# Eight experts served in the order of their counts, with a fixed room for each place of that order

## The chip, the cores and the metric

One core of one Trainium2 chip runs the whole kernel. The metric is the device time of the launch in microseconds (us). Times are medians over several launches of the same build. PE is the matrix engine (PEld its weight loads), DVE the vector engine, ACT the scalar engine, POOL the general engine that also issues indirect gathers, and SP the engine that issues plain DMA transfers.

## What is computed

Three layers, one behind the other. First a retention attention (4 batches, 8 heads, 576 positions, head size 64). Its output, 2304 tokens of 512 numbers, goes through a mixture of 8 experts of which each token uses the best two, and the result of that through a wide layer with `h * cos(h)`.

```python
logits = x @ w_gate                                   # 2304 x 8
noisy = logits + np.log1p(np.exp(x @ w_noise)) * noise
top2 = np.argpartition(-noisy, 2, axis=1)[:, :2]
top2_w = softmax(noisy[top2])
for e in range(8):
    for k in range(2):
        mask = top2[:, k] == e                        # how many: known only at run time
        h = np.maximum(x[mask] @ w1[e], 0.0)          # 512 -> 1024
        out[mask] += top2_w[mask, k, None] * (h @ w2[e])
h = out @ w_in                                        # 512 -> 2048
return (h * np.cos(h)) @ w_out                        # 2048 -> 512
```

Which tokens go to which expert, and how many, depends on the data. Together there are 4608 assignments, 576 for each expert on average.

## The kernel before, in words

**Numbers.** Each fp32 product is made from split values: a number is a high part and a low part, and one product takes three matmul passes (high by high, and the two mixed ones, `PASSES`). Weights arrive as units of 128x1024 fp32 (512 KB) in three staging buffers. `load_unit` (L273, on SP) asks for the next one, `split_unit` makes the high part on ACT (L286) and the low part on DVE (L287) and then asks for another. An expert has eight units, a0 to a3 of `w1` and b0 to b3 of `w2`.

**Attention and routing.** Twenty tiles run through attention. `routing(gi)` works beside it on four groups of tiles and finds, for each token, its two experts, their weights and its place within each expert. The last group ends with the tables of all experts: `ptab` to `gidx` (L668, whole rows of expert 0) and `gf` (L672), which a matmul spreads (L531) into `gidx4` (L683) for the gathers by quarter rows. Behind them two small matmuls (L686, L687) give the counts `cnt` (L688), from which `ntot` (L691) is the number of extra turns for tokens beyond an expert's room.

**Experts.** Every expert has a room of fixed size: `CAP = 616` columns, tokens being columns of the matmuls. A room is worked as two groups: group 0 with 256 columns (320 for expert 0) and group 1 with the rest, 360 (296 for expert 0). The number of columns is part of the instruction, so all of the room is computed, whether it holds tokens or not. `layer1(e, g)` makes 8 steps of 12 matmuls (L817), `layer2(e, g)` 4 steps of 24 (L838), so that a group takes 192 matmuls and an expert 384. Tokens are brought by gathers on POOL (`gather`, L730 and L736) and turned on PE (`turn`, L784). Between the steps of one expert stand the gathers and turns of the next, the splitting of its weights, and some steps of `cg`, which first computes `slot` (where each token's two results lie, `final_slots`, L1080 to L1110) and then prepares the last layer's weights (`convs`). The results go to DRAM as `ys` (L851 full blocks of 32 rows, L855 the rest of a room).

**Extra turns.** `overflow` (L995) reads `ntot` into a register and runs one turn of 128 tokens for each that does not fit a room. It stands between expert 0's first half and expert 0's second.

**The end of the experts.** The last expert (7) runs layer 1 and layer 2 of group 0, then `fetch(0)` starts 16 gathers from `ys` (L1171) for the first two blocks of tokens; these read only the rows up to the end of expert 7's group 0 (`FIRST`). Beside them PE runs group 1 of expert 7. `turn2(0)` weighs and adds the fetched rows (L1189, L1190), and `mlp1` (L1211 to L1229) and `mlp2` (L1241) follow for each of nine pairs of blocks.

**What sets the order.** Nothing is planned at run time. The order on every engine is that of the program, and the small work beside the matmuls is put in by hand-written lists of step numbers (`CG_1`, `CG_2`, `TURN_AT` and others).

Of the kernel before, what the change touches and what calls it, by code (L numbers as in the profile page):

```python
# [27 lines left out]
NTILE = B * NC  # L28
# [3 lines left out]

CAP = 616
NB = 5
CUT0, CUT = 320, 256
ROOM = (CUT0, CAP - CUT)
XB = (N - 512) // 128
YR = E * CAP
RB = N // 128
# [76 lines left out]
def constants():  # L116
    gam = 1.0 - 2.0 ** (-5.0 - np.arange(H, dtype=np.float64))
    pos = np.arange(S, dtype=np.float64)
    up = gam[:, None] ** pos[None, :] / np.sqrt(D)
    dn = gam[:, None] ** (-pos[None, :])  # L120
    dq = np.zeros((128, HP, 128), np.float32)
    gs = np.zeros((128, NC - 1, HP), np.float32)
    for hp in range(HP):
        for s in range(2):
            dq[s * 64:(s + 1) * 64, hp] = up[2 * hp + s, :128]
            for c in range(1, NC):
                gs[s * 64:(s + 1) * 64, c - 1, hp] = gam[2 * hp + s] ** START[c]
# [17 lines left out]
    xb[:, 0] = CAP  # L145
# [8 lines left out]
    small = np.concatenate([xb, io, base, k[:, None], k[:, None] // 32, tok, it], 1)  # L154

    spread = np.zeros((128, 4, 128), np.float32)
    for g in range(4):
        spread[:, g] = k[:, None] == g * 32 + (k % 32)[None, :]
    return {"c_dq": dqs, "c_big": big.astype(np.float32), "c_small": small.astype(np.float32),
            "c_spread": spread.reshape(128, -1), "c_zero": np.zeros((128, DM), np.float32)}  # L160
# [3 lines left out]
       ("strict", 128)]  # L164
SMALL = [("xb", E * XB), ("io", E), ("base", GN * E), ("pi", 1), ("pa", 1), ("tok", NTILE), ("it", E * RB)]

# [44 lines left out]
def moe_kernel(ctx, tc, x, out, dbg=None, phases="ABC"):  # L211
# [35 lines left out]
    cnt = con.tile([128, E], F32, name="cnt")  # L247
    ntot = con.tile([128, 1], I32, name="ntot")
    cbias = con.tile([128, 2], F32, name="cbias")
    beat = con.tile([1, 1], F32, name="beat")  # L250
# [3 lines left out]

    units = []
    for e in range(E):
        units += [(f"a{j}", x["w1"][4 * (e or E) + j], [128, DC, 256]) for j in range(4)]
        units += [(f"b{j}", x["w2"][4 * e + j], [128, 2, DM]) for j in range(4)]
# [3 lines left out]
    state.update(load=0, split=0, a=wpa)  # L262

# [114 lines left out]
    run = rt.tile([128, E], BF, name="run")  # L378
    adj = rt.tile([128, E], BF, name="adj")
    ptab = ps.tile([128, E * RB], F32, name="ptab")  # L380
    lgs = []
# [152 lines left out]
    ranked, begun = [0], []  # L534

    def routing(gi):

# [143 lines left out]
        if gi == len(GRP) - 1:  # L681
            pq = spread_out(gf.rearrange("p e n -> p (e n)"), "ph", PHB)
            vec.tensor_scalar(gidx4, pq, 4.0, sl["pa"], op0=OP.mult, op1=OP.add)  # L683
            yield
            pn = ps.tile([128, E], F32, name="ph", bufs=PHB)
            nc.tensor.matmul(pn, ones, run, start=True, stop=False)  # L686
            nc.tensor.matmul(pn, ones, adj, start=False, stop=True)  # L687
            vec.tensor_copy(cnt, pn)  # L688
            xf = rt.tile([128, E * XB], F32, name="xf", bufs=1)
            vec.tensor_tensor(ev(xf), ev(sl["xb"]), cnt[:, :, None].to_broadcast([128, E, XB]), op=OP.is_lt)  # L690
            vec.tensor_reduce(ntot, xf, axis=AX.X, op=OP.add)  # L691
            yield
# [31 lines left out]
    def gather(e, blk, early=False):  # L724
# [9 lines left out]
        else:  # L734
            ix = egid[:, blk:blk + 1] if early else gidx[:, e * RB + blk:e * RB + blk + 1]
            nc.gpsimd.indirect_dma_start(out=t.rearrange("p a d -> p (a d)"), out_offset=None,  # L736
# [8 lines left out]
    def width(e, g):  # L745
        cut = CUT if e else CUT0
        return CAP - cut if g else cut

    def places(e, blk):

        cut = CUT if e else CUT0
        c0, c1 = blk * 128, min(blk * 128 + 128, CAP)
        if c0 < cut:
# [73 lines left out]
    def layer2(e, g, early=False):  # L827
# [4 lines left out]
        for c in range(DC):  # L832
# [13 lines left out]
            if c < DC - 1:  # L846
                yield
        r0 = e * CAP + g * width(e, 0)
        for a in range(4):
# [222 lines left out]
    def final_slots():  # L1072
# [11 lines left out]
        for e in range(1, E):  # L1084
# [16 lines left out]
        V.scalar_tensor_tensor(ov, ei, float(CAP - N), vf, op0=OP.mult, op1=OP.add)
        V.tensor_tensor(slot.rearrange("p k t -> p (k t)"), a, ov, op=OP.add)
        yield
# [55 lines left out]

    FIRST = (E - 1) * CAP + 256  # L1160

# [198 lines left out]
```

## Time and profile before

| | |
|---|---|
| median of 3 runs | 980.35 us |
| the three runs | 980.35, 976.11, 986.68 us |
| the profiled execution | 986.75 us |
| its span in the trace | 985.0 us |
| its mean granted clock of TensorE | 0.988 |
| PE busy | 954.1 us (97%) |
| PEld busy | 894.9 us (91%) |
| DVE busy | 681.9 us (69%) |
| POOL busy | 485.6 us (49%) |
| ACT busy | 371.8 us (38%) |

The profiled execution is one execution, and 6.4 us longer than the median of the three runs. The share of busy time is a mean over stages that have different limits, so a stage has to be read by itself. Attention takes the first 145 us or so, the experts the time to about 570 us, the last layer the rest.

### The profile page before, as it was taken

What the parts mean: (1) busy time and instruction counts of PE and PEld (TensorE: products, weight loads), DVE (VectorE), ACT (ScalarE), POOL (GpSimd) and SP (SyncE); (2) the same over time, 40 slices, a digit from 0 to 9 for tenths busy, and PEclk for the clock granted to TensorE, in tenths of its full rate; (3) what the DMA queues carried; (4) which work ended last, traced back from release to release, by engine and by line L of the source; (5) the groups of instructions that cost most, each with busy time, mean ns of one, the idle gap of its engine ahead of it and who ended that gap; (6) DMA issues with size and microseconds to landing.
All of it is one profiled execution on the core that took longest, in us unless ns stands there. A gap on an engine that the chain in (4) does not pass through costs nothing.

```text
span 985.0 us, 18025 instructions
## 1 busy us (share of the span) xinstructions
PE 954.1 (97%) x6853; PEld 894.9 (91%) x6853; DVE 681.9 (69%) x1366; ACT 371.8 (38%) x659; POOL 485.6 (49%) x549
## 2 busy tenths in 40 slices
PE   8988988999999999999999899999999999999998
PEld 6776888999999999999999897989898998989897
DVE  4799875586878878686964378767484848566671
ACT  2422413341414232332333255435353535344451
POOL 6453114461818365473812537474654637473621
PEclk9998997999999999999999999999999999999999
DMA  9987495476758667686835342110101010111110
GB/s 348 283 280 211 117 356 168 129 220 172 240 165 238 210 194 218 171 259 167 252 95 155 122 134 89 36 36 33 55 15 51 20 46 25 44 32 40 30 23 22
DMA packets 79353, 135.39 MB, mean 137 GB/s; under 512 B 13025, under 2 KB 43105, under 8 KB 79265
## 3 DMA queue, kind: packets, MB, share of 16 engines
q1 hardware_dynamic: 69648, 113.74, 37.3%
q0 software_dynamic: 9472, 20.20, 7.3%
q8 instruction: 55, 0.90, 0.4%
q10 hardware_dynamic: 144, 0.27, 0.1%
q14 instruction: 34, 0.27, 0.1%
HBM read 106.25 MB, written 35.26 MB: 144 GB/s over the span
## 4 chain that ended last, share of the span: by engine, by line
PE 84%; DVE 6%; DMA 4%; issue 2%; POOL 1%; another core or an unknown queue 1%; ACT 1%; SPq 1%; DVEq 0%; ACTq 0%; POOLq 0%
PE py L1241 18%; PE ph L838 12%; PE ph L817 10%; PE ph L1211 10%; PE pt L817 8%; PE pt L1211 6%; PE ptab L817 4%; PE pt L838 3%; PE ptab L1211 3%; PE ptab L838 3%; DMA st<-w 2%; PE ph L446 1%; PE py L474 1%; PE py L488 1%
## 5 line engine op out<-in xcount | busy, mean ns | idle before, releaser
L1171 POOL DMA_INDIRECT y<-ys,slot x144 | 139.3, 967 | 53.9 <-issue 25.8
L1229 POOL TENSOR_TENSOR gl<-t,gh 128x512 fp32r<-128x512 f32 x67 | 87.0, 1300 | 136.4 <-issue 95.1
L730 POOL DMA_INDIRECT rows<-xs,gidx x132 | 134.8, 1021 | 35.0 <-issue 28.1
L743 POOL COPY beat<-hh 1x1 f32<-1x1 f32 x120 | 55.4, 462 | 154.7 <-ACT hh L822 150.6
L838 PE MATMUL ph<-hh,hb 128*128 128x360 f32 (+2 forms) x312 | 95.8, 307 | 1.7 <-issue 1.7
L838 PE MATMUL ph<-hh,lb 128*128 128x360 f32 (+2 forms) x312 | 96.1, 308 | 0.4 <-issue 0.4
L838 PE MATMUL ph<-hl,hb 128*128 128x360 f32 (+2 forms) x312 | 95.9, 307 | 0.6 <-issue 0.5
L1190 DVE SCALAR_TENSOR_TENSOR y<-y,wts,y 128x128 f32<-128x128 f32 x72 | 39.1, 579 | 55.4 <-DMA y<-ys,slot 46.0
L1217 DVE TENSOR_SCALAR t<-t 128x512 f32<-128x512 f32 x72 | 35.0, 486 | 49.3 <-ACT t L1216 49.3
L1219 DVE TENSOR_SCALAR t<-t 128x512 int32<-128x512 int32 x72 | 66.9, 930 | 2.5
L761 ACT ACTIVATE xh<-xt 128x512 fp32r<-128x512 f32 (+1 forms) x33 | 20.3, 616 | 114.4 <-DVE xt L769 107.1
L1222 ACT ACTIVATE t<-t,cbias 128x512 f32<-128x512 f32 x72 | 52.0, 722 | 29.0 <-DVE t L1219 27.8
L1241 PE MATMUL py<-ld,gh 128*128 128x512 f32 (+1 forms) x152 | 57.9, 381 | 3.7 <-POOL ld L287 2.5
L838 PEld LDWEIGHTS ph<-hh,hb 128*128 128x128 f32 x312 | 59.1, 189 | 2.1 <-issue 2.1
L838 PEld LDWEIGHTS ph<-hh,lb 128*128 128x128 f32 x312 | 59.1, 189 | 1.7 <-issue 1.7
L838 PEld LDWEIGHTS ph<-hl,hb 128*128 128x128 f32 x312 | 59.2, 190 | 0.1
L1241 PE MATMUL py<-hb,gh 128*128 128x512 f32 (+1 forms) x152 | 58.3, 384 | 0.0
L1241 PE MATMUL py<-lb,gh 128*128 128x512 f32 (+1 forms) x152 | 58.3, 383 | 0.0
L1241 PE MATMUL py<-hb,gl 128*128 128x512 f32 (+1 forms) x152 | 58.2, 383 | 0.0
L1241 PE MATMUL py<-hd,gh 128*128 128x512 f32 (+1 forms) x152 | 57.5, 378 | 0.0
L1241 PE MATMUL py<-hd,gl 128*128 128x512 f32 (+1 forms) x152 | 57.5, 378 | 0.0
L287 DVE TENSOR_TENSOR la<-st,ha 128x1024 fp32r<-128x1024 f32 x36 | 44.8, 1244 | 12.2 <-ACT ha L286 11.8
(308 smaller groups left out, 2657.5 us busy)
## 6 DMA issues: line engine op xcount, KB each, us to landing
st<-w SPq DMA_DIRECT2D x64, 512.0 KB
kv<-kv SPq DMA_DIRECT2D x16, 512.0 KB
ci<-wi SPq DMA_DIRECT2D x16, 512.0 KB
wc<-cy SPq DMA_DIRECT2D x32, 256.0 KB
ci<-wo SPq DMA_DIRECT2D x16, 512.0 KB
st<-wc SPq DMA_DIRECT2D x16, 512.0 KB
ys<-c_zero SPq DMA_DIRECT2D x7, 1024.0 KB
qr<-qt SPq DMA_DIRECT2D x20, 256.0 KB
```

What stands on the lines that cost most here:

```text
L287: lo_engine.tensor_tensor(lo.rearrange("p a b -> p (a b)"), st, hi.bitcast(F32).rearrange("p a b -> p (a b)"), op=OP.subtract)
L730: nc.gpsimd.indirect_dma_start(out=t[:, g, :], out_offset=None, in_=xs.rearrange("n (a d) -> (n a) d", a=4), in_offset=bass.IndirectOffset ...
L743: nc.gpsimd.tensor_copy(beat, src.bitcast(F32))
L817: nc.tensor.matmul(p[:, :n], w[a][:, dc, (f % 2) * 128:(f % 2 + 1) * 128], XE[e, g][b][:, dc, :n], start=(i == 0), stop=(i == 3 * DC - 1))
L838: nc.tensor.matmul(p[:, :n], w[a][:, f % 2, c * 128:(c + 1) * 128], HE[e, g][b][:, f, :n], start=(i == 0), stop=(i == 3 * FC - 1))
L1171: nc.gpsimd.indirect_dma_start(out=t[:, g, :], out_offset=None, in_=(ys if i else ys[:FIRST]).rearrange("n (a d) -> (n a) d", a=4), in_off ...
L1190: nc.vector.scalar_tensor_tensor(y0[:, g], y1[:, g], w1, y0[:, g], op0=OP.mult, op1=OP.add)
L1211: nc.tensor.matmul(p[:, f, :], w[a][:, dc, f * 128:(f + 1) * 128], X2[i][b][:, dc, :], start=(k == 0), stop=(k == 3 * DC - 1))
L1219: nc.vector.tensor_scalar(t.bitcast(I32), t.bitcast(I32), 0x7FFFFFFF, None, op0=OP.bitwise_and)
L1222: nc.scalar.activation(t, t, AF.Sin, scale=-1.0, bias=cbias[:, 1:2])
L1229: (nc.gpsimd if i or g > 4 else nc.vector).tensor_tensor(fl(gl), T[g], fl(gh.bitcast(F32)), op=OP.subtract)
L1241: nc.tensor.matmul(ps_[tb][:, :c1 - c0], parts[f // 2][b][:, f % 2, tb * 128:(tb + 1) * 128], w[a][:, f % 2, c0:c1], start=(f + k == 0), s ...
```

## The change

Expert 0 is still served first. The other seven are ranked on the chip by their counts, the largest first, and served in that order. Place `i` of the order has a fixed room `CAPS[i]`, and its results start at row `BASE[i]` of `ys`. Group 0 keeps its 256 columns (320 at place 0), so group 1 has 296, 360, 344, 336, 328, 320, 312 and 304 columns at the places 0 to 7.

Since the place of an expert is known only when the last routing group ends, the weights of the places 1 to 7 are loaded from an address held in a register: SP reads seven numbers (`order`), and the units that were due before that are held back (`owed`, three of them) and asked for then. The gather tables are permuted to the order of the places by a product with `hot` (1 where a place and an expert meet) and a sum. `final_slots` looks up the room and the first row of each token's expert in two more products and sums.

```diff
-CAP = 616
+CAPS = (616, 616, 600, 592, 584, 576, 568, 560)
+BASE = tuple(sum(CAPS[:i]) for i in range(E))
...
-YR = E * CAP
+YR = sum(CAPS)
...
+    tie = np.broadcast_to(np.where(e8, 7 - e8, 1 << 20)[None], (128, E))
+    place = np.broadcast_to(np.concatenate([CAPS, BASE])[None], (128, 2 * E))
...
+    expert = {0: 0}
+    def unit(name, e, j):
+        if not e:
+            return x[name][4 * (E if name == "w1" else 0) + j]
+        return x[name][bass.ds(expert[e] * 4 + j, 1)].rearrange("u p c -> (u p) c")
...
         u = state["load"]
         if u >= len(units):
             return
+        if u // 8 < E and u // 8 not in expert:
+            state["owed"] += 1
+            return
         state["load"] += 1
         st = stage.tile([128, 1024], F32, name="st")
-        nc.sync.dma_start(st, units[u][1])
+        src = units[u][1]
+        nc.sync.dma_start(st, src() if callable(src) else src)
...
+    def rank_experts():
...
+        pn = ps.tile([128, E], F32, name="ph", bufs=PHB)
+        nc.tensor.matmul(pn, ones, run, start=True, stop=False)
+        nc.tensor.matmul(pn, ones, adj, start=False, stop=True)
+        key, at_, sq = tl("key", [E]), tl("at_", [E]), tl("sq", [E, E])
+        vec.tensor_copy(cnt, pn)
+        vec.scalar_tensor_tensor(key, cnt, 8.0, sl["tie"], op0=OP.mult, op1=OP.add)
+        yield
+        vec.tensor_tensor(sq, row(key), column(key), op=OP.is_gt)
+        vec.tensor_reduce(at_, sq, axis=AX.X, op=OP.add)
+        yield
+        vec.tensor_tensor(hot, row(at_), column(sl["io"]), op=OP.is_equal)
+        vec.tensor_tensor(sq, hot, row(sl["io"]), op=OP.mult)
+        vec.tensor_reduce(order, sq, axis=AX.X, op=OP.add)
+        yield
+        for e in range(1, E):
+            expert[e] = nc.values_load(order[0:1, e:e + 1], engines=[mybir.EngineType.SP], min_val=1, max_val=E - 1)
+        for _ in range(state["owed"]):
+            load_unit()
...
+        vec.tensor_copy(ev(sl["xb"])[:, :, 0], cb2[:, 0])
+        xf = tl("xf", [E * XB])
+        vec.tensor_tensor(ev(xf), ev(sl["xb"]), column(cnt, XB), op=OP.is_lt)
+        vec.tensor_reduce(ntot, xf, axis=AX.X, op=OP.add)
...
+            yield from rank_experts()
             gf = rt.tile([128, E, NB], F32, name="gf", bufs=1)
...
+            gs = rt.tile([128, E, NB, E], F32, name="gs", bufs=1)
+            vec.tensor_tensor(gs, hot[:, :, None, :].to_broadcast([128, E, NB, E]),
+                              gf.rearrange("p e n -> p n e")[:, None].to_broadcast([128, E, NB, E]), op=OP.mult)
+            vec.tensor_reduce(gf, gs, axis=AX.X, op=OP.add)
+            vec.tensor_copy(whole, gf[:, 1, :WHOLE1])
...
         cut = CUT if e else CUT0
-        return CAP - cut if g else cut
+        return CAPS[e] - cut if g else cut
...
+        of_expert(a, me[:, :E])
+        yield
+        room, start = tl("room", [128, K2]), tl("start", [128, K2])
+        of_expert(room, cb2[:, 0])
+        yield
+        of_expert(start, cb2[:, 1])
+        yield
...
-    FIRST = (E - 1) * CAP + 256
+    FIRST = BASE[-1] + 256
```

SP around the end of routing, in the program before. `st` is a staging buffer for weights, `c_zero` a tile of zeros that clears `ys`, `y` the results of expert 0's group 0.

```order
L273 DMA st<-w 128x1024
L370 DMA ys<-c_zero 512x1x512
L273 DMA st<-w 128x1024
L370 DMA ys<-c_zero 512x1x512 x3
L273 DMA st<-w 128x1024
L370 DMA ys<-c_zero 512x1x512 x2
L273 DMA st<-w 128x1024
L370 DMA ys<-c_zero 512x1x512
L851 DMA ys<-y_1883 32x10x128 x4
L995 TENSOR_LOAD ntot
```

SP at the same place, now.

```order
L294 DMA st<-w 128x1024
L391 DMA ys<-c_zero 512x1x512 x7
L917 DMA ys<-y_1881 32x10x128 x4
L588 TENSOR_LOAD order
L588 ISA x2
...
L294 ISA
L294 DMA st<-w 128x1024
L294 ISA
L294 DMA st<-w 128x1024
L294 ISA
L294 DMA st<-w 128x1024
L1061 TENSOR_LOAD ntot
```

The three weight loads behind the first have moved past the clearing of `ys` and the write of expert 0's results, and behind seven reads of `order` (one read and two register instructions each). Each load now has a register instruction of its own.

DVE at the end of the last routing group, before: the tables, the counts, and then `d`, with which the softmax weights begin.

```order
L668 TENSOR_SCALAR gidx<-ptab 128x144
L672 TENSOR_SCALAR gf<-ptab 128x40
L678 CAST vs<-vi 128x2x4
L680 CAST eix<-ix 128x4 x2
L683 TENSOR_SCALAR gidx_85<-ph,cs 128x160
L688 COPY cnt<-ph 128x8
L690 TENSOR_TENSOR xf<-cs,cnt 128x112
L691 TENSOR_REDUCE ntot<-xf 128x1
```

DVE at the same place, now: between `gidx` and `gf` stand the fifteen instructions from the counts to `ntot`, of which some are shown.

```order
L735 TENSOR_SCALAR gidx<-ptab 128x144
L577 COPY cnt<-ph 128x8
L578 SCALAR_TENSOR_TENSOR key<-cnt,cs 128x8
L580 TENSOR_TENSOR sq<-key 128x64
...
L585 TENSOR_REDUCE order<-sq 128x8
...
L599 TENSOR_TENSOR xf<-cs,cnt 128x112
L600 TENSOR_REDUCE ntot<-xf 128x1
L740 TENSOR_SCALAR gf<-ptab 128x40
L743 TENSOR_TENSOR gs<-hot,gf 128x320
L745 TENSOR_REDUCE gf<-gs 128x40
L746 CAST whole<-gf 128x2
...
L757 TENSOR_SCALAR gidx_85<-ph,cs 128x160
```

`gidx`, which expert 0 needs, stays first. `gidx_85` (the table for the quarter rows) is now behind the whole ranking.

PE in expert 6, where layer 1 goes from group 0 to group 1, before (`pt` and `ptab` are accumulators, `xh` and `xl` the split tokens, `ha` and `la` the split weights).

```order
L817 MATMUL pt<-xh_5666,la_5671 128x256 x4
L817 MATMUL pt<-xl_5667,ha_5670 128x256 x4
L817 MATMUL ptab<-xh_5748,ha_5536 128x360 x4
L817 MATMUL ptab<-xh_5748,la_5537 128x360 x4
L817 MATMUL ptab<-xl_5749,ha_5536 128x360 x4
```

PE there, now.

```order
L883 MATMUL pt<-xh_5755,la_5760 128x256 x4
L883 MATMUL pt<-xl_5756,ha_5759 128x256 x4
L883 MATMUL ptab<-xh_5837,ha_5625 128x312 x4
L883 MATMUL ptab<-xh_5837,la_5626 128x312 x4
L883 MATMUL ptab<-xl_5838,ha_5625 128x312 x4
```

The matmuls and their order are the same. Those of group 1 are narrower, 312 columns for 360 at this place.

## Rows read from the trace of the kernel before

**Rows 1.** The page, part 1: busy time, share of the span, instructions.
```profile
PE 954.1 (97%) x6853; PEld 894.9 (91%) x6853; DVE 681.9 (69%) x1366; ACT 371.8 (38%) x659; POOL 485.6 (49%) x549
```

**Rows 2.** Windows: stretch, length, then PE, PEld, DVE, ACT, POOL busy; clock, DMA, GB/s.
```profile
402.21:456.19 53.98, 53.98 (x387) 53.98 (x386) 42.13 (x78) 17.40 (x29) 28.91 (x36) 1.00 0.71 214
145.00:150.00 5.00, 0.18 (x4) 0.08 (x3) 2.20 (x11) 0.21 (x1) 2.52 (x3) 0.85 1.04 333
150.00:155.00 5.00, 3.83 (x15) 3.03 (x16) 1.71 (x3) 1.50 (x3) 0.95 (x1) 0.50 0.13 47
550.00:570.00 20.00, 17.32 (x89) 15.76 (x87) 7.13 (x18) 3.52 (x9) 7.93 (x11) 0.91 0.27 82
```

**Rows 3.** Chain of waits, expert 5: start, us, what; groups 0 and 1 apart.
```profile
402.21 2.87 PE pt L817 x24
...
415.71 5.94 PE ph L817 x36
...
429.54 5.45 PE ph L838 x48
...
444.38 11.82 PE ph L838 x72
```

**Rows 4.** Chain of waits, expert 0's group 1, 296 columns wide.
```profile
161.40 4.94 PE ph L817 x36
...
175.60 9.83 PE ph L838 x72
```

**Rows 5.** Chain of waits, last layer, a stretch of matmuls with 512 columns.
```profile
643.40 22.10 PE py L1241 x96
```

**Rows 6.** Timeline of DVE, end of routing: start, us, what, idle before.
```profile
143.63 0.27 DVE L668 TENSOR_SCALAR gidx<-ptab 128x144 int32<-128x144 f32 x1
...
145.19 0.38 DVE L683 TENSOR_SCALAR gidx<-ph,cs 128x160 int32<-128x160 f32 x1 [0.96 <-PE ph L687]
145.49 0.15 DVE L688 COPY cnt<-ph 128x8 f32<-128x8 f32 x1
...
152.04 0.42 DVE L762 TENSOR_TENSOR xl<-pt,xh 128x256 fp32r<-128x256 f32 x1 [4.14 <-ACT xh L761]
```

**Rows 7.** Timeline of DVE, the product of `final_slots`.
```profile
162.27 0.48 DVE L1090 TENSOR_TENSOR mo<-oh,me 128x320 f32<-128x320 f32 x1
```

**Rows 8.** Timeline of PE, end of routing.
```profile
144.06 1.08 PE L531 MATMUL ph<-gf,spread 128*128 128x40 f32 x8 [0.54 <-DVE gf L672]
...
150.47 1.97 PE L784 MATMUL pt<-ident,rows 128*128 128x128 f32 x8 [5.29 <-DMA rows<-xs,gidx]
```

**Rows 9.** Chain of waits, the gathers of expert 0.
```profile
144.64 5.78 DMA rows<-xs,gidx
```

**Rows 10.** Line 995, SP's read of `ntot`: ns least, median, most; first and last start.
```profile
L995 SPq TENSOR_LOAD <-ntot x1: 482/482/482, 146.3 to 146.3; - x1
...
L995 SPq FUSED_REGOPS  x1: 202/202/202, 146.8 to 146.8; - x1
```

**Rows 11.** Timeline of SP, expert 0's results.
```profile
143.74 2.21 SPq L851 DMA_DIRECT2D ys<-y  x4
```

**Rows 12.** Timeline of ACT, the first split of expert 1's weights.
```profile
163.40 1.05 ACT L286 ACTIVATE ha<-st 128x1024 fp32r<-128x1024 f32 x1
```

**Rows 13.** Timeline of SP, expert 7's results of group 0.
```profile
533.51 1.86 SPq L851 DMA_DIRECT2D ys<-y  x4
```

**Rows 14.** Timeline of POOL, first and last of the 16 gathers for the last layer.
```profile
538.19 0.98 POOL L1171 DMA_INDIRECT y<-ys,slot  x1 [2.34 <-DMA ys<-y]
...
558.72 0.94 POOL L1171 DMA_INDIRECT y<-ys,slot  x1 [0.30 <-issue]
```

**Rows 15.** Timeline of all engines, the end of expert 7.
```profile
561.52 0.55 DVE L843 STREAM_TRANSPOSE y<-ptab 128x352 f32<-128x352 f32 x1 [11.54 <-remote]
...
567.82 1.10 DVE L1190 SCALAR_TENSOR_TENSOR y<-y,wts,y 128x128 f32<-128x128 f32 x4
...
570.39 0.73 PE L1211 MATMUL pt<-x2h,hc 128*128 128x256 f32 x4 [0.36 <-ACT x2h L761]
```

More of the change, by code (lines that the diff above doesn't have):

```diff
@@ L1 @@
 from contextlib import ExitStack
+from functools import partial
 from itertools import chain
@@ L31 @@
 GC = FF // 128
-CAP = 616
+CAPS = (616, 616, 600, 592, 584, 576, 568, 560)
+BASE = tuple(sum(CAPS[:i]) for i in range(E))
 NB = 5
 CUT0, CUT = 320, 256
-ROOM = (CUT0, CAP - CUT)
+ROOM = (CUT0, max(CAPS) - CUT)
 XB = (N - 512) // 128
-YR = E * CAP
+YR = sum(CAPS)
 RB = N // 128
@@ L153, in constants @@
     it = np.broadcast_to(np.arange(E * RB)[None], (128, E * RB))
-    small = np.concatenate([xb, io, base, k[:, None], k[:, None] // 32, tok, it], 1)
+    tie = np.broadcast_to(np.where(e8, 7 - e8, 1 << 20)[None], (128, E))
+    place = np.broadcast_to(np.concatenate([CAPS, BASE])[None], (128, 2 * E))
+    small = np.concatenate([xb, io, base, k[:, None], k[:, None] // 32, tok, it, tie, place], 1)
     spread = np.zeros((128, 4, 128), np.float32)
@@ L164 @@
        ("strict", 128)]
-SMALL = [("xb", E * XB), ("io", E), ("base", GN * E), ("pi", 1), ("pa", 1), ("tok", NTILE), ("it", E * RB)]
+SMALL = [("xb", E * XB), ("io", E), ("base", GN * E), ("pi", 1), ("pa", 1), ("tok", NTILE), ("it", E * RB), ("tie", E),
+         ("place", 2 * E)]
 def layout(q, k, v, moe_w_gate, moe_w_noise, moe_noise, moe_w1, moe_w2, moe2_w_in, moe2_w_out):
@@ L248, in moe_kernel @@
     ntot = con.tile([128, 1], I32, name="ntot")
+    cb2 = con.tile([128, 2, E], F32, name="cb2")
+    whole = con.tile([128, WHOLE1], I32, name="whole")
     cbias = con.tile([128, 2], F32, name="cbias")
@@ L255, in moe_kernel @@
     units = []
+    expert = {0: 0}
[3 more added lines that the diff above has]
+        return x[name][bass.ds(expert[e] * 4 + j, 1)].rearrange("u p c -> (u p) c")
     for e in range(E):
-        units += [(f"a{j}", x["w1"][4 * (e or E) + j], [128, DC, 256]) for j in range(4)]
-        units += [(f"b{j}", x["w2"][4 * e + j], [128, 2, DM]) for j in range(4)]
+        units += [(f"a{j}", partial(unit, "w1", e, j), [128, DC, 256]) for j in range(4)]
+        units += [(f"b{j}", partial(unit, "w2", e, j), [128, 2, DM]) for j in range(4)]
     wcf = wc.bitcast(F32)
@@ L261, in moe_kernel @@
     loaded, W = {}, {}
-    state.update(load=0, split=0, a=wpa)
+    state.update(load=0, split=0, owed=0, a=wpa)
     def x_tiles(g):
@@ L379, in moe_kernel @@
     adj = rt.tile([128, E], BF, name="adj")
+    hot = rt.tile([128, E, E], F32, name="hot")
+    order = rt.tile([128, E], I32, name="order")
     ptab = ps.tile([128, E * RB], F32, name="ptab")
@@ L534, in moe_kernel, with tl, row, column @@
     ranked, begun = [0], []
+    def rank_experts():
+        vec = nc.vector
+        def tl(name, shape):
+            return rt.tile([128, *shape], F32, name=name, bufs=1)
+        def row(ap, n=E):
+            return ap[:, None, :].to_broadcast([128, n, E])
+        def column(ap, n=E):
+            return ap[:, :, None].to_broadcast([128, E, n])
+        pn = ps.tile([128, E], F32, name="ph", bufs=PHB)
[16 more added lines that the diff above has]
+            load_unit()
+        vec.tensor_tensor(sq, column(at_), row(sl["io"]), op=OP.is_equal)
+        for i in range(2):
+            sp = tl(f"sp{i}", [E, E])
+            vec.tensor_tensor(sp, sq, row(sl["place"][:, i * E:(i + 1) * E]), op=OP.mult)
+            vec.tensor_reduce(cb2[:, i], sp, axis=AX.X, op=OP.add)
+        yield
[4 more added lines that the diff above has]
+        yield
     def routing(gi):
@@ L683, in routing @@
             vec.tensor_scalar(gidx4, pq, 4.0, sl["pa"], op0=OP.mult, op1=OP.add)
[L684 to L691, printed above, removed]
             yield
@@ L734, in gather @@
         else:
-            ix = egid[:, blk:blk + 1] if early else gidx[:, e * RB + blk:e * RB + blk + 1]
+            ix = (egid if early else whole if e else gidx)[:, blk:blk + 1]
             nc.gpsimd.indirect_dma_start(out=t.rearrange("p a d -> p (a d)"), out_offset=None,
@@ L746, in width @@
         cut = CUT if e else CUT0
-        return CAP - cut if g else cut
+        return CAPS[e] - cut if g else cut
     def places(e, blk):
         cut = CUT if e else CUT0
-        c0, c1 = blk * 128, min(blk * 128 + 128, CAP)
+        c0, c1 = blk * 128, min(blk * 128 + 128, CAPS[e])
         if c0 < cut:
@@ L847, in layer2 @@
                 yield
-        r0 = e * CAP + g * width(e, 0)
+        r0 = BASE[e] + g * width(e, 0)
         for a in range(4):
```

19 lines of the change are left out of this document (10 added, 9 removed).

## The prediction

> **What bounds the kernel now.** I read the page's busy times first, then windows, then the chain of waits inside one expert, and last the timelines at the two ends of the expert stage. The page gives PE 97% of the span and PEld 91% [rows 1]. Those are means. The window over expert 5 is the one that counts: in 53.98 us PE and PEld are both busy for 53.98 us, at a granted clock of 1.00 (the 2.4 GHz level), while DVE has 42.13 us of work, ACT 17.40 and POOL 28.91, and the DMA engines are used at 0.71 [rows 2]. The chain in that window is made of matmuls alone [rows 3]. So inside the experts the end moves with the length of the matmuls and with nothing else, as long as the others keep up. The change makes matmuls narrower. What must be found is what a column costs, how many columns go, and where the time that PE saves is really saved.
>
> **What a column costs.** Expert 5's layer 1 takes 5.94 us for 36 matmuls of 360 columns, 0.1650 us each, and layer 2 11.82 us for 72, 0.1642 [rows 3]. Expert 0's second group has 296 columns: 4.94 us for 36, 0.1372, and 9.83 us for 72, 0.1365 [rows 4]. The difference over 64 columns is 0.0278 and 0.0277 us, that is 0.433 ns a column. The line is straight to both sides: group 0's 256 columns take 5.45 us for 48, 0.1135 [rows 3], and 0.1642 less 104 columns at 0.433 is 0.119; 512 columns take 22.10 us for 96, 0.230 [rows 5], and 0.1642 plus 152 columns is 0.230. All new widths, 304 to 344, lie between rows that exist. Each matmul brings a weight load of the same size as now, and the row at 256 columns shows that a load a matmul fits into 0.1135 us, below the 0.140 that 304 columns want. So the loads are no floor here.
>
> One page speaks against this price. By the Trainium skill, "TensorE: Matmul & The Clock Gate", section "Back-to-back issue gap", a stream of weight loads and matmuls settles at about 81 ns for 128 columns and 131 ns for 512. That would make an estimate of 0.13 ns a column and the gain below 4.0 us; the rows at 256, 296, 360 and 512 disagree with it, and I go by them.
>
> **The columns that go.** Places 0 and 1 keep 616. Places 2 to 7 lose 16, 24, 32, 40, 48 and 56 columns, all in group 1, where an expert has 96 + 96 = 192 matmuls. Places 2 to 6 lose 160 columns: 160 x 192 x 0.433 ns = 13.3 us. Place 7 loses 56 x 192 x 0.433 ns = 4.7 us of PE time.
>
> **Place 7: I count none of its 4.7 us.** The last layer's first matmul needs tokens fetched from `ys`. Those gathers start after expert 7's group 0 is written (issue at 533.51 [rows 13]); sixteen of them run back to back on POOL, the first at 538.19, the last ending at 559.66 [rows 14]. Group 0 has 256 columns before and after, so this chain keeps its length. Behind the last gather come a landing, the weighted sum (1.10 us [rows 15]) and a turn and a split; I estimate 5 us, so the first matmul of the last layer could start near 564.5. PE goes on to group 1 of expert 7 just ahead of that write, near 533.0, with 192 matmuls at 0.1646: 533.0 + 31.6 = 564.6. The two are level now. With 304 columns PE would be done at 559.9 and wait 4.6 us for the same gathers. In this execution DVE stood 11.54 us until 561.52 for something that the trace calls remote, the last sums came at 567.82 and the first matmul at 570.39 [rows 15], and PE was busy for only 17.32 of 20 us there [rows 2]; that would hide place 7's gain even more. Bounds: 0 and 4.7 us; I take 0.
>
> **The ranking, on DVE.** Between `gidx` and `gf` come fifteen small instructions, one more cast and two of 128x320. The nearest rows: 0.15 us for 8 columns and 0.38 for 160 [rows 6], 0.48 for 128x320 (`final_slots`' product [rows 7]). Fifteen at 0.15 to 0.38 make 2.3 to 5.7, two at 0.48 make 1.0. The first of them waits for the two count matmuls, which moved ahead; the idle time of such a wait was 0.96 us [rows 6]. From 143.90, when `gidx` is done, `gf` comes at 148.2 to 151.5, the spreading matmuls (1.08 us [rows 8]) end 149.3 to 152.6. That is beside a wait: PE stands 5.29 us until 150.47 for expert 0's gathers [rows 8], whose 5.78 us begin at 144.64 [rows 9], and they need only `gidx`, which stays first. In PE's order the spread stands ahead of the turns of the gathered rows, so what reaches beyond 150.47 is a loss: nothing at the low price, 2.1 us at the high one. The held-back loads also leave the DMA queues to the gathers, which move at 333 GB/s with the rest there [rows 2], so up to 1 us may come back. I take 0, for the middle of that chain ends at 151 and DVE next has something to do for expert 0 at 152.04 [rows 6]. Range -1 to +2.1.
>
> **The loads, on SP.** `order` is written about 2 us after the counts, near 146.0; SP ends its `ys` writes at 143.74 + 2.21 = 145.95 [rows 11]. A read of a register costs 0.482 + 0.202 us [rows 10], with the second register instruction at the same price 0.89: seven take 4.8 to 6.2 us, so the three held-back loads go out at 151 to 152.2. They are 1.57 MB: 4.7 us at 333 GB/s, and the stretch 150 to 155 had only 47 GB/s in it [rows 2]. All have landed by 157. The first is split at 163.40 [rows 12]. Cost 0, with 6 us to spare. Queued behind the reads on SP stand the read of `ntot` and the first conversion loads, which nobody on PE waits for. Later loads each get one register instruction, 0.2 us [rows 10] on a queue that has no part in the chain of expert 5 [rows 3].
>
> **The rest.** `final_slots` gets two more products and sums, 4 x 0.48 = 1.9 us of DVE in the first experts, where DVE has 12 us free in 54 [rows 2]; the conversions move two steps later and one step is left for the end of place 6. `ys` rows beyond whole blocks of 32 change from 8 per expert to 8, 24, 16, 8, 0, 24, 16: four transfers fewer, on SP. Together 0.
>
> **The sum.** 13.3 + 0 + 0 + 0 = 13.3 us less. The profiled execution, at 986.75, would become 973.4; it is 6.4 above the median, part of which the stall near 561 explains. From the median: 980.35 - 13.3 = **967.0 us**.
>
> **The rivals.**
> - *Place 7 pays too.* If the gathers come earlier in an undisturbed execution than I read from this one, all 18.0 us are kept: 962.4. For it: the estimate of 5 us behind the last gather is mine. Against: the gathers alone end at 559.66 [rows 14], when the narrower PE work would end. Chance 0.14.
> - *Other engines take half back.* A place of 312 columns lasts 54.0 - 48 x 192 x 0.433 ns = 50.0 us, with the same splits, turns, conversions and weights. DVE at 42.1 us would be at 84%, DMA at 0.71 x 54 / 50 = 0.77 [rows 2]. Single waits for a split, a table step or the late last conversion could return 6 or 7 us: 974. Chance 0.16.
> - *Width does not count.* If the weight loads, busy throughout [rows 2], set the pace, the gain is 0 and the time 980; the rows at 256 and 296 columns speak against it. By the Trainium skill, "Perfetto Trace Analysis", section "Identifying the Most-Contended Engine", it is the busy share of the weight loads that tells how near PE is to its limit, and they are at 91%; the trace agrees with that share but its pace goes with width. With prices in between, 976. Chance 0.03.
> - *The ranking makes expert 1's weights late (slower).* Should one read of `order` cost as much as the wait for a transfer does, 5.78 us [rows 9], for 0.68, seven end at 146.0 + 40.5 = 186.5, and the first load lands at 188. The split that ACT meets at 163.40 [rows 12] then holds the activations of expert 0 behind it, and PE with them: 25 us, 967 + 25 = 992. It begins to cost at (163.4 - 146.0 - 1.6) / 7 = 2.3 us a read, and decides where 13.3 us more make the loss as large as the gain, at 4.2 us a read. Against: the same read of `ntot` took 0.48 [rows 10]. Chance 0.03.
> - *The change does not hold its rooms (slower).* If a count is above its smaller room, an extra turn runs: gathers (5.78 us [rows 9]), 4.2 MB of weights at 333 GB/s (12.6 us [rows 2]), 192 matmuls at no more than 0.1135 (21.8 us [rows 3]), one behind the other, 40 us: 1007. The reference's arithmetic on its default draw gives sorted counts 614, 606, 591, 587, 570, 566, 539 and 535, of which none exceeds its place; another draw can. Chance 0.04.
>
> **How the numbers follow.** The forecast has the remaining 0.60. The medians shown reach from 976.11 to 986.68, so a median of three is known to about 4 us; with the bounds of the ranking (-1 to +2.1) the forecast's case spans 960 to 973. Adding the two neighbours, 962 and 974 with the same spread, the range is 957 to 978. A measurement of this kernel can tell about 1%, 9.8 us: faster is below 970.5, slower above 990.2. Below 970.5 lie about 0.8 of the forecast's case, nearly all of place 7's, a quarter of the half-gain: 0.48 + 0.13 + 0.04 = 0.65. Slower are the last two rivals: 0.07. The rest, 0.28, is within 1%.
>
> **What the changed profile would show.** The chain in place 5 should show 36 matmuls of layer 1 in about 5.3 us (320 columns, 0.1477 each) for 5.94, and a place 5 of 50.7 us for 53.98, PE still without gaps. If the weight loads bound, the 36 would still take 5.9. At the end of place 7 PE should wait 4 to 5 us ahead of line 1211's successor for fetched rows; if it does not, place 7 paid. After routing the wait for expert 0's rows should end within 2 us of 5.8 after the gathers began, and the first split of place 1's weights should wait for nothing; if it waits for `st`, the reads were dear. I am wrong if PE shows gaps for DVE or for weights in places 4 to 6, or if any instruction of the extra turns runs.

## The result, and the profile after

The changed kernel takes 970.88 us (median of 4 runs, 969.09 to 971.43) against 981.91 for the kernel before in the same comparison: a ratio of 0.9887, 95% interval 0.9847 to 0.9927. A second measurement, beside other kernels, gave 0.9888 (0.9856 to 0.9919). So some 11 us are gone, where 13.3 were forecast. The profiled execution took 970.36 us, span 968.5.

Busy times on the page, answering [rows 1]:

```profile
PE 939.1 (97%) x6853; PEld 882.7 (91%) x6853; DVE 678.6 (70%) x1381; ACT 370.1 (38%) x659; POOL 483.7 (50%) x549
```

The number of matmuls is the same and PE is as full as before; its busy time is 15 us shorter. Windows after routing and over place 5, columns as in [rows 2]:

```profile
145.00:150.00 5.00, 1.60 (x8) 1.60 (x9) 3.48 (x15) 0.00 (x0) 1.99 (x3) 0.66 0.92 252
150.00:155.00 5.00, 4.35 (x24) 3.98 (x24) 3.09 (x11) 1.71 (x4) 1.89 (x2) 0.65 0.74 239
155.00:160.00 5.00, 5.00 (x39) 5.00 (x38) 3.14 (x14) 1.25 (x3) 2.48 (x6) 1.00 0.96 375
...
395.16:446.32 51.16, 51.16 (x387) 51.16 (x386) 40.83 (x75) 16.90 (x29) 27.91 (x36) 1.00 0.75 224
```

Place 5 is 51.16 us long for 53.98, and PE and PEld are still busy without a gap. DVE's work of 40.83 us and the DMA share of 0.75 did not stand in the way. The chain of waits, answering [rows 3] and [rows 4], shows the pieces of place 5 and, first, the start of expert 0's second group:

```profile
153.58 3.52 PE pt L883 x24
...
408.43 5.28 PE ph L883 x36
...
420.75 5.76 PE ph L904 x48
...
435.78 10.54 PE ph L904 x72
```

Here is the gain, and what is missing from it. Layer 1 of group 1 (L883, 320 columns) takes 5.28 us for 5.94, layer 2 of group 1 (L904) 10.54 for 11.82: 0.1467 and 0.1464 us a matmul, which is the line of 0.433 ns a column. But layer 2 of group 0, whose 256 columns nobody changed, takes 5.76 us for 48 where it took 5.45.

The end of routing, in the timelines of DVE, PE, SP and ACT in this order ([rows 6, 8, 11, 12]):

```profile
147.86 0.48 DVE L745 TENSOR_REDUCE gf<-gs 128x40 f32<-128x320 f32 x1
...
148.40 1.93 PE L555 MATMUL ph<-gf,spread 128*128 128x40 f32 x8 [5.27 <-DVE gf L745]
150.13 1.95 PE L850 MATMUL pt<-ident,rows 128*128 128x128 f32 x8
...
150.29 1.60 SPq L294 DMA_DIRECT2D st<-w  x3
...
160.75 1.05 ACT L307 ACTIVATE ha<-st 128x1024 fp32r<-128x1024 f32 x1
```

The ranking has taken the place of the gathers as what PE waits for: 5.27 us for `gf`, where it waited 5.29 for rows. The turns then start without a wait. SP's seven reads of `order`, by line:

```profile
L588 SPq TENSOR_LOAD <-order x7: 262/262/627, 145.5 to 149.5; - x7
```

They are done by 150.0, the three held-back loads go out at 150.29, and the first split needs them at 160.75. The end of place 7, waits of PE from 500 to 560 us (total, times, longest):

```profile
PE pt L1285 <- ACT x2h L827: 6.1, 1, 6.1
```

Before the last layer's first matmul PE now stands 6.1 us for fetched tokens: what place 7's narrower matmuls saved is waited away. The wait also costs clock. Windows over the first 10 us of the last layer, columns as in [rows 2], of the change and of `b_again` (the kernel before, a second time), where PE had not waited:

```profile
552.46:562.46 10.00, 10.00 (x69) 10.00 (x70) 4.62 (x8) 3.88 (x6) 2.01 (x3) 0.81 0.52 123
562.38:572.38 10.00, 10.00 (x86) 10.00 (x85) 4.28 (x8) 3.47 (x5) 1.88 (x2) 1.00 0.54 134
```

The granted clock is 0.81 for 1.00, so part of the stretch ran at the lower level, 1.2 GHz, and it holds 69 matmuls for 86.

**Stage by stage.** The table gives, for each profiled kernel, the time from one stage's first matmul to the next one's, in us, worked out from the starts of matmuls in the traces. "routing" is from `gidx` on DVE to the first matmul of expert 0's group 1, "half 0" from there to place 1, "rest" from the last layer's first matmul to the end of the span. The experiments' kernels are explained below.

| kernel | routing | half 0 | 1 | 2 | 3 | 4 | 5 | 6 | 7 | rest | sum of 1 to 6 |
|---|---|---|---|---|---|---|---|---|---|---|---|
| before | 10.59 | 31.04 | 54.84 | 53.98 | 53.98 | 53.98 | 53.98 | 53.98 | 60.38 | 414.6 | 324.7 |
| b_again | 10.34 | 31.02 | 54.84 | 53.98 | 53.98 | 53.98 | 53.98 | 53.98 | 54.40 | 414.4 | 324.7 |
| after | 10.48 | 28.63 | 55.35 | 53.06 | 52.43 | 51.94 | 51.16 | 50.42 | 55.88 | 416.0 | 314.4 |
| a_again | 10.48 | 30.92 | 55.35 | 53.06 | 52.43 | 51.94 | 51.16 | 50.42 | 55.01 | 416.0 | 314.4 |
| all616 | 10.47 | 31.14 | 55.35 | 54.49 | 54.49 | 54.49 | 54.49 | 54.49 | 54.98 | 414.7 | 327.8 |
| all616_pad | 10.47 | 28.64 | 54.87 | 53.98 | 53.98 | 53.98 | 53.98 | 53.98 | 55.81 | 414.6 | 324.8 |
| pad64 | 10.48 | 30.90 | 54.87 | 52.98 | 52.29 | 51.72 | 50.96 | 50.34 | 54.92 | 414.3 | 313.2 |
| p7wide | 10.47 | 30.92 | 55.35 | 53.06 | 52.43 | 51.94 | 51.16 | 50.42 | 54.47 | 416.5 | 314.4 |
| asc | 10.48 | 31.16 | 50.56 | 50.41 | 51.17 | 51.95 | 52.43 | 53.06 | 56.45 | 416.6 | 309.6 |
| asc_pad | 10.47 | 31.04 | 50.48 | 50.32 | 50.54 | 51.72 | 52.30 | 52.98 | 60.01 | 414.9 | 308.3 |
| g0narrow | 10.47 | 30.96 | 55.35 | 53.06 | 52.99 | 53.02 | 53.02 | 53.00 | 55.31 | 416.6 | 320.4 |
| reads_x4 | 10.47 | 34.12 | 55.35 | 53.06 | 52.43 | 51.94 | 51.16 | 50.42 | 55.49 | 416.0 | 314.4 |

Places 1 to 6 repeat to a hundredth of a microsecond from one execution of a kernel to the next, so differences there can be read from one trace each. Half 0 and place 7 vary between executions of the same kernel: half 0 is 28.6 or 31 (34.1 in `reads_x4`), place 7 54.4 to 56.5 or 60. From before to after places 1 to 6 lose 10.4 us. Of the other 6 of the 16.5 us between the two spans, 4.5 are the 60.38 of before and 2.4 are half 0; the stage called rest is 1.4 longer.

That last figure need not be chance. Rest is 416.0 to 416.6 in all six profiles of kernels that have narrowed rooms and no pad, and 414.3 to 414.9 in the six others; `after` and `a_again` agree, and so do before and `b_again`. The windows from 45 to 55 us into the last layer, behind PE's waits for the last converted weights, show a difference that goes with it, here `after` and `pad64`:

```profile
597.46:607.46 10.00, 8.08 (x43) 6.93 (x42) 4.50 (x6) 3.23 (x8) 4.05 (x3) 0.83 0.20 67
597.88:607.88 10.00, 8.12 (x57) 7.37 (x56) 5.77 (x9) 3.27 (x7) 4.04 (x3) 1.00 0.19 67
```

The granted clock there is 0.83 in each of those six profiles and 1.00 in the others. So the change, as it stands, may pay some 1.5 us in the last layer; whether these come with the kernel or by chance is not shown by one profile each.

### The profile page after: what moved, and what is told of

It reads as the page before. It is cut to its first block, busy times and chain, and to the rows that moved or that the text cites. A ratio compares the mean times of both kernels' runs of the same rounds, so it can differ in the third digit from the quotient of the medians.

```text
span 968.5 us, 18167 instructions
## 1 busy us (share of the span) xinstructions
PE 939.1 (97%) x6853; PEld 882.7 (91%) x6853; DVE 678.6 (70%) x1381; ACT 370.1 (38%) x659; POOL 483.7 (50%) x549
## 4 chain that ended last, share of the span: by engine, by line
PE 89%; POOL 3%; DVE 3%; DMA 2%; issue 1%; SPq 1%; ACT 1%; DVEq 0%; POOLq 0%
PE py L1315 19%; PE ph L904 12%; PE ph L1285 11%; PE ph L883 10%; PE pt L883 8%; PE pt L1285 7%; PE ptab L883 4%; PE ptab L1285 4%; PE pt L904 4%; PE ptab L904 3%; PE ph L470 2%; POOL y L1245 1%; PE py L904 1%; PE py L512 1%; PE py L498 1%
## 5 line engine op out<-in xcount | busy, mean ns | idle before, releaser
L1245 POOL DMA_INDIRECT y<-ys,slot x144 | 142.8, 992 | 47.0 <-issue 28.5
L809 POOL COPY beat<-hh 1x1 f32<-1x1 f32 x120 | 51.1, 426 | 149.7 <-ACT hh L888 148.2
L904 PE MATMUL ph<-hl,hb 128*128 128x256 f32 (+8 forms) x312 | 93.7, 300 | 0.0
L904 PE MATMUL ph<-hh,lb 128*128 128x256 f32 (+8 forms) x312 | 93.6, 300 | 0.0
L904 PE MATMUL ph<-hh,hb 128*128 128x256 f32 (+8 forms) x312 | 93.6, 300 | 0.0
L1264 DVE SCALAR_TENSOR_TENSOR y<-y,wts,y 128x128 f32<-128x128 f32 x72 | 39.1, 573 | 61.6 <-DMA y<-ys,slot 50.6
L1291 DVE TENSOR_SCALAR t<-t 128x512 f32<-128x512 f32 x72 | 35.0, 486 | 50.3 <-ACT t L1290 50.3
L827 ACT ACTIVATE xh<-xt 128x512 fp32r<-128x512 f32 (+7 forms) x33 | 19.6, 593 | 116.9 <-DVE xt L835 102.4
L904 PEld LDWEIGHTS ph<-hh,hb 128*128 128x128 f32 x312 | 58.8, 188 | 0.0
L904 PEld LDWEIGHTS ph<-hh,lb 128*128 128x128 f32 x312 | 58.7, 188 | 0.0
L904 PEld LDWEIGHTS ph<-hl,hb 128*128 128x128 f32 x312 | 58.7, 188 | 0.0
L308 DVE TENSOR_TENSOR lb<-st,hb 128x1024 fp32r<-128x1024 f32 x35 | 43.6, 1245 | 10.7 <-ACT hb L307 10.1
```

Of the source, the lines that this page charges most:

```text
L308: lo_engine.tensor_tensor(lo.rearrange("p a b -> p (a b)"), st, hi.bitcast(F32).rearrange("p a b -> p (a b)"), op=OP.subtract)
L809: nc.gpsimd.tensor_copy(beat, src.bitcast(F32))
L904: nc.tensor.matmul(p[:, :n], w[a][:, f % 2, c * 128:(c + 1) * 128], HE[e, g][b][:, f, :n], start=(i == 0), stop=(i == 3 * FC - 1))
L1245: nc.gpsimd.indirect_dma_start(out=t[:, g, :], out_offset=None, in_=(ys if i else ys[:FIRST]).rearrange("n (a d) -> (n a) d", a=4), in_off ...
L1264: nc.vector.scalar_tensor_tensor(y0[:, g], y1[:, g], w1, y0[:, g], op0=OP.mult, op1=OP.add)
```

## The experiments

Intervals are those of the ratio to the kernel before; the kernels under one number were measured side by side on one chip, those under different numbers on different chips.

**1. Where are the buffers, and what do ranking and place 7 cost?** The matmuls whose pace changed have the same size and order as before. One thing that differs is where their data lie: the tables that the change adds among the constants push the weights and group 0's tokens up by 192 bytes a partition, while group 0's results of layer 1 (`hh`, `hl`) stay (group 1's move down by 320). `pad64` adds 64 unused bytes:

```diff
     cbias = con.tile([128, 2], F32, name="cbias")
+    con.tile([128, 16], F32, name="pad")
```

> An unused tile of 64 bytes per partition is added among the constants, so that every buffer allocated behind them (weights, tokens of group 0) lies 256 bytes further up than in the kernel before instead of 192. Theory 1 (the place of the buffers sets the pace of layer 2's 256-column matmuls): 48 of them take 5.45 us again for 5.70 in places 1 to 6, and the time falls by about 6 x 0.5 = 3 us, from 970.9 to 968. Rival (the pace belongs to the new order of work or to the loads addressed by register): 5.70 and 970.9 stay.

`all616` takes the narrow rooms away and leaves everything else of the change:

```diff
-CAPS = (616, 616, 600, 592, 584, 576, 568, 560)
+CAPS = (616,) * 8
```

> All eight rooms 616: ranking, held-back loads and register addresses alone, no column dropped. Theory 1: against before, +0.5 us in each of places 1 to 6 from the slower layer 2 and -2.4 us from the clock that is back earlier after routing, together about +1, 980 to 984; stage by stage each place 1 to 6 takes 54.5 us. Rival (the ranking or the loads cost time of their own): above 986, with gaps on PE after routing or in place 1.

`p7wide` gives only place 7 its old width:

```diff
-CAPS = (616, 616, 600, 592, 584, 576, 568, 560)
+CAPS = (616, 616, 600, 592, 584, 576, 568, 616)
```

> Place 7 gets 616 columns again, the others as in the change. Theory (the gathers for the last layer set its start, not PE): the same time as the change, 970.9 within 1.5 us, and PE's wait of 6.1 us for the fetched tokens shrinks to about 1.5. Rival (place 7's width is on the path): 4.7 us more, 975.6.

`b_again` is the kernel before, unchanged.

> The kernel before, one more profiled execution. Theory 1: 48 layer-2 matmuls of 256 columns take 5.45 us in places 1 to 6 in every execution. Rival (the pace varies from launch to launch): 5.70 in this one. And if the 11.5 us in which DVE stood at the end of expert 7 belong to that one execution, expert 7 takes 54 to 56 us here up to the last layer's first matmul, for 60.2.

Measured: `pad64` 968.61 us, ratio 0.9868 (0.9844 to 0.9893); `all616` 984.58, 1.0037 (1.0015 to 1.0058); `p7wide` 972.69, 0.9908 (0.9889 to 0.9928); `b_again` 978.62 in its one run. The chain of waits, layer 2 of group 0 at places 1 and 2, of `b_again`:

```profile
211.60 5.45 PE ph L838 x48
...
265.58 5.45 PE ph L838 x48
```

of `all616`:

```profile
213.26 5.70 PE ph L904 x48
...
267.75 5.70 PE ph L904 x48
```

and of `pad64` (its lines stand one lower for the added one):

```profile
213.17 5.45 PE ph L905 x48
...
266.43 5.66 PE ph L905 x48
```

The pace does not vary from launch to launch: `b_again` has 5.45 everywhere, as before. `all616` has 5.70 with no column dropped, so the slow pace does not come from the narrow rooms. The pad brings 5.45 back at place 1, behind a group 1 of 360 columns, but 5.65 elsewhere: half right. Its median is 2.3 us below the change's, which was not measured beside it; its places 1 to 6 give 1.2 of that.

`all616` has no gap on PE that before has not; it costs 3 us at places 1 to 6, all of it the pace. The -2.4 us at half 0 that I had put to its account, and so the 980 to 984, did not come: half 0 is 31.14 there.

`p7wide` decides place 7. Its narrow width was worth 4.7 us of PE time, yet place 7 takes 54.47 us with 616 columns and 55.88 and 55.01 with 560. The narrow place is not the shorter one. PE's wait of 6.1 us is gone from the list, where about 1.5 were expected to be left. The total, 972.69, lies 1.8 us above the expected 970.9 and 2.9 below the rival's 975.6, and the ratio, 0.9908, has an interval that overlaps that of the change. Nor does a wide place 7 in `b_again` (54.40) differ; the 60.38 of the first profile of before were that execution's stall [rows 15].

**2. The order turned round, the pad alone, and the change again.** `a_again` is the changed kernel, unchanged.

> The changed kernel once more, beside the other kernels of this call. Theory: 970.9 within 1.5 us; the first 24 matmuls after routing take 5.5 to 6.0 us, as in all other traces so far, not the 3.52 of its first trace, so that this piece of 2.3 us is chance and no part of the change. Rival (the ranking brings the clock back earlier): 3.5 us again.

If place 7's width is worth nothing, it should have the widest room. `asc` serves the smallest count first:

```diff
-CAPS = (616, 616, 600, 592, 584, 576, 568, 560)
+CAPS = (616, 560, 568, 576, 584, 592, 600, 616)
...
-    tie = np.broadcast_to(np.where(e8, 7 - e8, 1 << 20)[None], (128, E))
+    tie = np.broadcast_to(np.where(e8, 7 - e8, -(1 << 20))[None], (128, E))
...
-        vec.tensor_tensor(sq, row(key), column(key), op=OP.is_gt)
+        vec.tensor_tensor(sq, row(key), column(key), op=OP.is_lt)
```

> The order is turned round: the seven experts are served with the smallest count first, rooms 560, 568, 576, 584, 592, 600, 616 at the places 1 to 7. The same columns are dropped, but all of them at places 1 to 6, none at place 7. Theory (place 7 sets no time by its width, places 1 to 6 do, at 0.433 ns a column and matmul): 56 x 192 x 0.433 ns = 4.7 us less than the change, 966.2. Rival 1 (place 1, just behind routing, waits for weights or gathers when it is narrow): 970 to 971, with gaps on PE in place 1. Rival 2 (all columns count alike, wherever they go): 970.9.

`asc_pad` is `asc` with the 64 bytes of `pad64`.

> The turned order and the unused 64 bytes together. Theory: the two add up, 966.2 less what the pad saved at places with narrow second groups, about 1 us: 965. In the trace the 256-column layer 2 takes 5.65 us for 48 in places 1 to 6 (it took 5.45 with the pad only behind a second group of 360 columns).

`all616_pad` is `all616` with the 64 bytes.

> All rooms 616 and the unused 64 bytes: ranking, held-back loads and register addresses, with the buffers where they lay before (256 bytes further up). Theory 1 (what ranking seemed to cost is the place of the buffers): 5.45 us for 48 matmuls at all of places 1 to 6 and 981.5 within 1.5, 3 us less than with all rooms 616 alone. Rival (ranking and loads cost 3.4 us themselves): 984.6, and the pace stays at 5.70.

Measured: `a_again` 972.08 us, 0.9888 (0.9856 to 0.9919); `asc` 970.40, 0.9858 (0.9817 to 0.9899); `asc_pad` 965.83, 0.9809 (0.9771 to 0.9847); `all616_pad` 984.81, 1.0019 (0.9995 to 1.0042), with the kernel before at 983.79.

`all616_pad` settles the pace. It differs from `all616` by 64 unused bytes a partition, and places 1 to 6 go from 327.8 us back to 324.8, the 324.7 of before. The chain of waits at place 1:

```profile
210.80 5.45 PE ph L905 x48
```

So ranking, held-back loads and register addresses cost nothing at places 1 to 6, and the 3 us are the place of the buffers. The medians alone would not have told: 1.0037 and 1.0019 have overlapping intervals. The expected 981.5 missed by 3 us, but before stood 2.6 us higher on that chip.

`a_again`: the first matmuls of half 0, in the chain of waits, take

```profile
155.16 5.79 PE pt L883 x24
```

and not 3.52. Of twelve profiled executions ten show the long form and two (`after`, `all616_pad`) the short. The windows show that it is the clock. In `after` the granted clock is back at 1.00 (the 2.4 GHz level) in 155 to 160 (above); in before it was at 0.50 (the 1.2 GHz level) in 150 to 155 [rows 2], and then

```profile
155.00:160.00 5.00, 5.00 (x26) 5.00 (x25) 0.94 (x4) 0.62 (x2) 2.09 (x3) 0.63 0.80 247
```

so part of that stretch still ran at the lower level. In both PE had stood 5.3 us ahead of it. These 2.3 us are chance, since `after` and `a_again` are one kernel, and I was wrong to read them as the ranking's.

`asc` does at places 1 to 6 what was expected, 309.6 us for 314.4: 4.8 less, for 4.7 worked out. Over place 1, columns as in [rows 2], PE has no gap in 50.60 us, so rival 1 falls:

```profile
185.00:235.60 50.60, 50.60 (x394) 50.60 (x394) 38.32 (x73) 17.36 (x31) 25.08 (x36) 1.00 0.61 184
```

The total of `asc` alone would speak for rival 2 (970.9): it is only 1.7 us under `a_again`, with overlapping intervals, and leaves the amount open. In its profile place 7 took 56.45 us, 1.4 more than in `a_again`. With the pad places 1 to 6 are at 308.3, 6 us below the change, and `asc_pad` is faster than `a_again` beyond both intervals: the best version found, 1.9% faster than before. In its chain place 3, with a 256-column layer 2 behind a group of 320, came out at 5.45,

```profile
313.63 5.45 PE ph L905 x48
```

the other places at 5.65. What picks the pace at a given place is therefore not the width of 360 alone, as I had expected from `pad64`.

**3. How near are the held-back loads, and is there a floor under the width?** `reads_x4` reads each entry of `order` four times:

```diff
         for e in range(1, E):
-            expert[e] = nc.values_load(order[0:1, e:e + 1], engines=[mybir.EngineType.SP], min_val=1, max_val=E - 1)
+            for _ in range(4):
+                expert[e] = nc.values_load(order[0:1, e:e + 1], engines=[mybir.EngineType.SP], min_val=1, max_val=E - 1)
```

> Each of the seven entries of the order is read four times (28 reads of 0.64 us, 18 us for 4.5), so that the held-back loads go out near 163.5 us for 150.0. Theory of the prediction (the loads have some 6 us to spare before the first split of place 1's weights, and beyond that ACT and with it PE wait): the first unit lands 5 us after the split wants it, PE loses about 4 us ahead of place 1, 976. Rival (the loads are further off the path than that): no gap on PE, 971.

`g0narrow` takes the columns from group 0:

```diff
-        cut = CUT if e else CUT0
+        cut = (CAPS[e] - 360) if e else CUT0
...
-    FIRST = BASE[-1] + 256
+    FIRST = BASE[-1] + CAPS[-1] - 360
```

With it the first fetch reads only 200 rows of place 7, which holds for these counts but not for every draw.

> The same rooms, but the columns are taken from group 0 of places 1 to 7 (256, 240, 232, 224, 216, 208, 200) and group 1 keeps 360. Theory 1 (a column costs 0.433 ns at any width, and place 7's shorter group 0 lets the gathers for the last layer start earlier): the same 10 us at places 1 to 6 and some 4.7 us more at place 7, 966. Rival (below 256 columns the weight loads set the pace, 0.113 to 0.120 us a matmul): the matmuls of group 0 stay at 0.113 to 0.120, nothing is gained in places 2 to 7, 981.

Measured: `reads_x4` 974.63 us, 0.9929 (0.9901 to 0.9957); `g0narrow` 977.22, 0.9954 (0.9937 to 0.9971).

`reads_x4`, line 589, what ACT waited for, and ACT's timeline behind routing:

```profile
L589 SPq TENSOR_LOAD <-order x28: 260/263/636, 149.7 to 165.5; - x28
```

```profile
ACT ha L307 <- DMA st<-w: 2.5, 1, 2.5
```

```profile
166.03 0.72 ACT L889 ACTIVATE hh<-pt 128x296 fp32r<-128x296 f32 x2 [8.32 <-SPq L589]
```

The reads end at 166.0. Routing came 4.2 us later in this execution, so seven would have ended near 154.2; the loads are 11.8 us later for it, and half 0 grows from 30.9 to 34.1. Of the 11.8 us 3.2 are lost and 8.6, some 15 reads of 0.56 us, were room. The late load is not the only path, and not the first that waits. ACT's longest wait behind routing is for the reads themselves: the results of layer 1 (`hh`) of group 1, which are put where the routing's tables and `order` lay, stood 8.32 us until the last read ended. In the change the reads end at 150.0, and the first `hh` starts at 155.5 behind PE, so that this wait begins with reads some 5.5 us later. How the 3.2 us divide between the two waits is not shown.

`g0narrow`, the chain of waits of place 5, group 0 now 216 columns wide (L883 the first and, last, L904) and group 1 of 360 between them:

```profile
403.56 4.02 PE ph L883 x36
...
412.25 5.94 PE ph L883 x36
...
426.08 5.35 PE ph L904 x48
```

4.02 / 36 is 0.1117 us, 5.35 / 48 is 0.1115. The same 0.1115 to 0.112 stand at 240, 232, 224, 208 and 200 columns: that is the floor, and places 3 to 6 all take 53.0 us although each has fewer columns than the one before it. From 256 to 240 columns, 0.120 to 0.112 and 0.1187 to 0.1117, the line of the columns still held; below 240 nothing more is gained. Place 7's shorter group 0 gained nothing either, 55.31 us. The rival was right below 240 columns, with a floor a little under the row it was read from. Its "nothing is gained" was too strong: places 2 to 6 stand 1 us each under before, and the total is 977 for its 981.

## Why the prediction was right, and where its size was off

**The price of a column held.** 0.433 ns between 296 and 360 columns gives 0.1477 us at 320 for layer 1 and 0.1469 for layer 2; place 5 shows 0.1467 and 0.1464. By the starts of the matmuls, the narrowed groups of places 2 to 6 gave 13.7 us in all, for the 13.3 of the sum. `asc` confirms the price by moving columns: 4.8 us for 4.7. By the Trainium skill, "TensorE: Matmul & The Clock Gate", section "Back-to-back issue gap", 128 to 512 columns differ by 50 ns; the trace does not agree for these fp32 streams, where 296 to 360 alone differ by 28.

**Places 1 to 6 were sized at 13.3 us and brought 10.4.** The sum's step that failed is one it did not make: it took the matmuls of group 0 as unchanged because their number, width and order are. Their data had moved by 192 bytes, and layer 2 of group 0 went from 0.1135 to between 0.1187 and 0.120 us a matmul, 0.5 to 0.6 us at each of places 1 to 6. Over the six places that is 3.3 us, and 13.7 - 3.3 is the 10.4. `all616` against before shows 3.0 us at these places, `all616_pad` 0.03. The order of the program shows such a step nowhere, but the rows gave a hint, and the prediction passed over it where it calls the line straight to both sides. By its line 256 columns cost 0.119, and the 0.1135 of layer 2 lay below that; layer 1's 256 columns, 2.87 us for 24, took 0.1196 in the same [rows 3]. Two paces at one width stood there already.

**Place 7 at nothing: right.** PE waited 6.1 us where 4 to 5 were forecast, and `p7wide` shows that giving the width back costs no time in place 7. What the prediction left out is the clock behind that wait: the last layer's first 192 matmuls took 24.8 us in `after`, 25.5 in `pad64` and 23.0 in `b_again`. Most of it can come back: the 96 behind them took 24.3 us in `pad64` and 26.7 in `b_again`, because PE then waits less for the last converted weights. The rival that kept 18 us falls in the order of the change; turned round and padded, places 1 to 6 of `asc_pad` are 16.4 us shorter than before.

**The ranking at nothing: right**, and within its bounds. `gf` was done at 148.34 (148.2 to 151.5 forecast), and from `gidx` to the first matmul of expert 0's group 1 it is 10.48 us for 10.59 and 10.34. What PE waits for there has changed, how long has not. That the end of the ranking falls level with the gathers it replaced (5.27 and 5.29 us) is luck: at the high price of the forecast it would have cost 2.1.

**The loads on SP at nothing: right.** Seven reads took 4.5 us (4.8 to 6.2 forecast), and by `reads_x4` they could have ended 8.6 us later before half 0 grew (6 forecast). But the prediction saw only the path over the split; the nearer one, from the reads to `hh`, has 5.5 us and is not in it.

**The rivals.** That other engines take half back is not seen: place 5 has no gap, and the shortest places, 50.3 to 50.6 us in `asc` and `asc_pad`, have none either. That loads bind is not seen at 304 to 344 columns, where the time goes with the width; below 240 it no longer does, though no run shows that it is the weight loads that set the pace there. No extra turn ran.

**The range.** The times that the prediction calls medians (976.11 to 986.68) are three single runs, and the median of 980.35 that it started from came out at 981.91 with a fourth run. 1.6 of the 3.9 us between its 967.0 and the 970.88 are that start, the other 2.3 the smaller gain: 11.0 for 13.3.

## What to carry to other kernels

Price a narrower matmul from two widths of the same stream in the trace, find the width where the price stops (here 0.1115 us, near 240 columns), and count columns only where PE is what ends last; where a transfer chain ends last, put the widest piece there. A change that adds a few bytes ahead of other buffers moves them all, and a kernel that runs at PE's pace can pay for that: try a pad before judging the change. Where total times scatter by 1%, the lengths of single stages in the traces can still be exact to hundredths of a microsecond.

## What was not expected of the hardware

In places 1 to 6 a stream of 256-column fp32 matmuls settles at one of several paces, 0.1133, 0.1177, 0.1187 or 0.120 us each, and keeps it for all 96 of a layer. In layer 2 the pace depends on where the buffers lie (64 bytes changed 0.1187 to 0.1133 at six places of `all616`), and in kernels with narrowed rooms also on the place. Layer 1 kept its 0.120 wherever it had 256 columns, in all twelve profiles; there weights and tokens move by the same number of bytes, while in layer 2 the weights move and group 0's `hh` and `hl` stay. Shown is that the address matters. Whether it is the distance between the two that counts is not tested, and what makes place 3 of `asc_pad` different from its neighbours stays open.

In two stretches executions of one kernel differ by chance: the clock after routing (2.3 us), and at the end of place 7 a stall of 4 to 6 us in two of twelve profiles (before and `asc_pad`; `b_again` has none), where DVE stands 11.5 and 10.8 us for something that the trace only calls remote. In both it starts again 1.9 and 1.2 us behind the end of POOL's last gather (559.66 and 561.52; 545.40 and 546.57), while in the ten others it works beside the gathers. What it waits for was not found. For the 2 us in the last layer, chance and the kernel are both open.
